# A fused retention and gated MLP kernel: first block loaded and masked by pairs of heads, third and fourth block prepared at other places

## The chip, the cores and the metric

The kernel runs on one core of one Trainium2 chip. The metric is the device time of one execution in microseconds (us). The engines are named as the profile names them: PE is TensorE, DVE is VectorE, ACT is ScalarE, POOL is GpSimd, SP is SyncE, which here only issues DMAs. PE multiplies, the others copy, scale and round. Every engine works through its own instructions in order.

## The reference

```python
def _attn_ref(q, k, v):                       # (8, 8, 576, 64) each: batch, heads, sequence, head dim
    scores = scale * np.matmul(q, k.transpose(0, 1, 3, 2))
    gamma = 1.0 - 2.0 ** (-5.0 - np.arange(H, dtype=np.float32))
    rel = pos[:, None] - pos[None, :]
    Dmat = np.where(rel >= 0, gamma[:, None, None] ** rel[None, :, :], 0.0)
    ret = scores * Dmat[None, :, :, :]
    return np.matmul(ret, v).astype(np.float32)

def _moe_ref(x, w_in, w_out):                 # x: 4608 x 512, w_in: 512 x 2048, w_out: 2048 x 512
    h = x @ w_in
    g = h * np.cos(h)
    return (g @ w_out).astype(np.float32)
```

The heads' outputs are put side by side and are the rows `x` of the second function.

## The kernel before

**Blocks and windows.** The 4608 tokens are cut into 18 blocks of 256 tokens (`j`) for the attention, and into 9 windows of 512 tokens (`n`) for the MLP. The decay is split into a factor on q and one on k (`gq`, `gkp`, `gkc`), so that a plain triangular mask is left. For each block: SP loads q, k and v (`load`); q and k are scaled and rounded to bf16 (`scaled`, line 174); v is rounded (`round_v`, line 185); PE turns q and k (`transpose_pe`, line 225, for blocks 0 and 1, `turned`, line 210, for the rest) into PSUM, and ACT or DVE copy the result to `qkT` (lines 230, 216); PE forms the scores (lines 264, 302), DVE masks them (`masked`, lines 282, 311); PE forms the states that go on to later tokens (`sums_of`, lines 352, 335), which are added up in `s_all` and rounded in `sb` (line 394); PE forms the outputs from the block itself (`out_own`, line 420) and from the carried state (`out_carried`, line 447), and ACT rounds them into `x_of`.

**The MLP.** `mm1` (line 490) multiplies four tiles of `w_in` with the window, ACT takes the cosine (line 503), DVE multiplies (line 506). The second product of window 0 is written out in the loop over `order` (line 991); windows 1 to 8 use `mm2_seven` (line 610), which forms seven products in place of eight, and needs sums of weight quarters, `w_sums` (line 529, DVE), made once, during window 0.

**Order.** The order is written out by hand. The tile layer adds the semaphores, and each engine runs its list in this order. What matters here is the start and window 0:

- SP issues the loads of block 0 (k, q, v, 512 KB each), then k, q of block 1, and v of block 1 once its k has landed.
- POOL makes masks, issues the first quarter of `w_in` (a cast DMA), scales k of block 1, and then issues the other three quarters. `w_dma` lists the weight DMAs: 0 to 3 are `w_in`, 4 to 7 the quarters of `w_out`.
- Block 2's loads are held by `gate=w_dma[3]` until the last quarter of `w_in` has landed, block 3's by `gate=w_dma[6]`. The third quarter of `w_out` is held until the first has landed (`after(w_dma[-1], w_dma[4])`).
- In window 0 `mm1` runs eight groups. Group 0 and 3 need the first quarter of `w_in`, group 1 and 4 the second, 2 and 5 the third, 6 and 7 the last. The sums, outputs and carried part of block 1 lie between groups 0 and 2.
- The second product of window 0 has 64 steps. A list `todo` says ahead of which step something else is put in: the scaling of half of q of block 2 on DVE (20), its turning (28), its states and scores (40), the adding of its states (41), scaling of block 3 (`prep(3)`, 42, on POOL), weight sums (`w_sums`), block 2's outputs (54), block 3's turning (60). The product lies in banks "m" (two tiles, `two`), "n" and "st" of PSUM. Two tiles in "m" are copied out by ACT and DVE (line 1001) after step 55:

```python
for u in range(2 * (t == 1) if t < 2 else 1) if e == ET - 1 else ():
    ...
    (act, vec)[u % 2](ot[:, 0], pss[u])
```

The first group of window 1 writes bank "m" again (`banks_of[1]` begins with "m"). It can begin when both copies are done.

`warm(n, tag)` (line 235) runs n matmuls on zeros into a bank; nothing reads them.

Of the kernel before, what the change touches and what calls it, by code (L numbers as in the profile page):

```python
# [17 lines left out]
def kernel(  # L18
# [113 lines left out]
    def load(j, names="qkv", gate=None):  # L132
# [27 lines left out]
            tiles["f" + name, j] = f  # L160
        return i

    def scaled(eng, j, name, y):
        f = tiles["f" + name, j]
        if ("qks", j) not in tiles:
            tiles["qks", j] = nat.tile([P, 2, 2, HG, 2, D], BF16, tag="qks", name="qks")
        dst = tiles["qks", j][:, "qk".index(name), y]
        if name == "q" or j < NP_B:
            src = f[:, :, y, :]
            by = (gq if name == "q" else gkp)[:, j % PERQ, y, :]  # L170
        else:
            src = f[:, y]
            by = gkc[:, (2 * j + y) % PERK, :]
        return eng.tensor_tensor(  # L174
            out=dst.rearrange("p b a d -> p a b d"),
            in0=src.rearrange("p (a b) d -> p a b d", a=2),
            in1=by.rearrange("p (a b) -> p a b", a=2).unsqueeze(3).to_broadcast([P, 2, HG, D]),
            op=ALU.mult,
        )
# [5 lines left out]
            runs[y](vb[:, y], f[:, :, y, :] if j < NP_B else f[:, y])  # L185
        tiles["vb", j] = vb

    def prep(j):
        for name in "kq" if j < NP_B else "qk":
            for y in range(2):  # L190
                scaled(nc.gpsimd, j, name, y)

    def new_qkT(j):
        tiles["qkT", j] = nat.tile([P, 2, 2, HG, P], BF16, tag="qkT", name="qkT")
# [23 lines left out]
    def transpose_pe(j, name, bank, evac, ys=(0, 1)):  # L218
        if ("qkT", j) not in tiles:
            new_qkT(j)  # L220
        m = "qk".index(name)
        ps = psum.tile([P, len(ys), HG, P], BF16, tag=bank, name="tr")
        for u, y in enumerate(ys):
            for hg in range(HG):
                nc.tensor.transpose(
                    ps[:, u, hg, :],
                    tiles["qks", j][:, m, y, hg].rearrange("s a d -> s (a d)"),
                    ident,
                )
        evac(tiles["qkT", j][:, m, ys[0] : ys[-1] + 1], ps)  # L230

    def warm(n, tag):
        ps = psum.tile([P, 512], F32, tag=tag, name="idle")
        for _ in range(n):
            nc.tensor.matmul(ps, lhsT=zeros[:, :P], rhs=zeros, start=True, stop=True)
# [10 lines left out]
            return cols  # L246
        return cols.rearrange("p (r i) -> p r i", r=2)[:, :, c.i0 : c.i0 + n]

    def scores(j, banks):
        cs = chunks[j]  # L250
        kT = tiles["qkT", j]
        ret = retp.tile([P, 2, HG, 2, P], BF16, tag="ret", name="ret")
        if cs[0].pair:
            pss = [
                psum.tile([P, HG, 2, P], F32, tag=t, name="sc")
                if isinstance(t, str)
                else [psum.tile([P, HG, P], F32, tag=u, name="sc") for u in t]
                for t in banks
            ]
            order = [(c, y, he, hg) for hg in range(HG) for y in range(2) for he in range(2) for c in cs]  # L260
            mask = mask_p
            for c, y, he, hg in order:
                ps = pss[he]
                nc.tensor.matmul(
                    ps[y][c.rows, hg, :] if isinstance(ps, list) else ps[c.rows, hg, y, :],
                    lhsT=kT[he * D : he * D + D, 1, y, hg, c.rows],
                    rhs=q_cols(c, he, hg, c.n),
                    start=True,
                    stop=True,
                )  # L270

            def masked(he):
                if isinstance(pss[he], list):
                    for y in range(2):
                        nc.vector.tensor_tensor(
                            out=ret[:, he, :, y, :],
                            in0=pss[he][y],
                            in1=mask[:, y].unsqueeze(1).to_broadcast([P, HG, P]),
                            op=ALU.mult,
                        )  # L280
                    return
                nc.vector.tensor_tensor(  # L282
                    out=ret[:, he].rearrange("p b r i -> p b (r i)"),
                    in0=pss[he].rearrange("p b r i -> p b (r i)"),
                    in1=mask.rearrange("p r i -> p (r i)").unsqueeze(1).to_broadcast(
                        [P, HG, 2 * P]
                    ),
                    op=ALU.mult,
                )
        else:  # L290
            ret = ret.rearrange("p a b r i -> p (a b r i)")[:, : 2 * HG * P].rearrange(
                "p (a b y i) -> p a b y i", a=2, b=HG, y=2
            )
            if isinstance(banks[0], str):
                both = psum.tile([P, 2, HG, 2, HP], F32, tag=banks[0], name="sc")
                ps = [both[:, he] for he in range(2)]
            else:
                ps = [psum.tile([P, HG, 2, HP], F32, tag=t, name="sc") for t in banks[0]]
            for hg in range(HG):
                for c in cs:  # L300
                    for he in range(2):
                        nc.tensor.matmul(  # L302
                            ps[he][c.rows, hg, c.y, :],
                            lhsT=kT[he * D : he * D + D, 1, c.y, hg, c.rows],
                            rhs=q_cols(c, he, hg, c.n),
                            start=True,
                            stop=True,
                        )

            def masked(he):  # L310
                nc.vector.tensor_tensor(  # L311
                    out=ret[:, he].rearrange("p b y i -> p (b y) i"),
                    in0=ps[he].rearrange("p b y i -> p (b y) i"),
                    in1=mask_c.unsqueeze(1).to_broadcast([P, H, HP]),
                    op=ALU.mult,
                )

        tiles["ret", j] = ret
        return [lambda: masked(0), lambda: masked(1)]

    def sums_of(j, bank):
# [399 lines left out]
    def load_next(**kw):  # L721
        nonlocal loaded
        if loaded < NB:
            load(loaded, **kw)
            loaded += 1
# [31 lines left out]
            out=at, in0=at, in1=lng.unsqueeze(1).to_broadcast(list(at.shape)), op=ALU.mult  # L757
        )

    load(0, "kqv")  # L760
    k1 = load(1, "k")
    load(1, "q")
    load(1, "v", gate=k1)
# [19 lines left out]
            kpos_i[p0:, c0:c1, :], pattern=[[P, c1 - c0], [0, H]], base=base, channel_multiplier=1  # L783
        )
    nc.vector.memset(zeros, 0.0)
    warm(11, "n")
    for h in range(H):
        nc.vector.memset(lng[:, h : h + 1], math.log(gammas[h]))
    nc.vector.memset(ln_scale, math.log(scale))
# [34 lines left out]
        )  # L824
    vec, act = nc.vector.tensor_copy, nc.scalar.copy

    scaled(nc.vector, 0, "k", 0)
    scaled(nc.vector, 0, "k", 1)
    transpose_pe(0, "k", "n", act, (0,))
    transpose_pe(0, "k", "st", act, (1,))  # L830
    scaled(nc.vector, 0, "q", 0)
    scaled(nc.vector, 0, "q", 1)
    transpose_pe(0, "q", "a", act, (0,))
    transpose_pe(0, "q", "b", vec, (1,))
    w_dma = [load_w_in(0)]
    round_v(0, (act, act))
    warm(2, "m")
    for masked in scores(0, "ab"):
        masked()
    sums_of(0, "st")()()  # L840
    scaled(nc.gpsimd, 1, "k", 0)
    warm(3, "m")
    transpose_pe(1, "k", "n", act, (0,))
    scaled(nc.gpsimd, 1, "k", 1)
    w_dma += [load_w_in(e) for e in (512, 1024, 1536)]
    load_next(names="kqv", gate=w_dma[3])
    ps0 = psum.tile([P, DG, BK], F32, tag="m", name="ov")
    out_own(0, ps0)
    scaled(nc.vector, 1, "q", 0)
    scaled(nc.vector, 1, "q", 1)  # L850
    transpose_pe(1, "k", "st", vec, (1,))
    out_carried(0, ps0)
    act(x_of(0), ps0)
    nc.scalar.activation(sine, half_pi, ACTF.Sin, bias=0.0, scale=1.0)
    round_v(1, (act, nc.gpsimd.tensor_copy))
    warm(2, "n")
    transpose_pe(1, "q", "a", vec, (0,))
    transpose_pe(1, "q", "b", vec, (1,))
    warm(2, "n")
    for masked in scores(1, "ab"):  # L860
        masked()
    w_dma += [load_w_out(e) for e in (0, 4)]
    w_dma.append(load_w_out(8))
    after(w_dma[-1], w_dma[4])
    for y in range(2):
        scaled(nc.gpsimd, 2, "k", y)
    w_dma.append(load_w_out(12))
    scaled(nc.gpsimd, 2, "q", 0)
    load_next(names="kqv", gate=w_dma[6])
    load_next()  # L870
    prepared = 4

# [48 lines left out]
    for n in range(NT):  # L921
# [37 lines left out]
        if n == 0:  # L959
# [3 lines left out]
            pss += [psum.tile([P, DM], F32, tag=t, name="o") for t in ("n", "st")]  # L963
            todo = [
                (20, lambda: scaled(nc.vector, 2, "q", 1)),
                (28, lambda: turned(2, "a", (act, vec))),
                (28, lambda: round_v(2)),
                (40, lambda: adds.append(states_and_scores(2, "a", "b"))),
                (41, lambda: adds.pop()()()),
                (42, lambda: prep(3)),  # L970
                (57, load_next),
                (55, lambda: round_v(3, (act, act))),
                (54, lambda: outputs(2, "b")),
# [2 lines left out]
            todo += [  # L976
                (at, lambda x=x, e=e: w_sums(x, e, e + 4))
                for at, x, e in (
                    (2, 5, 0), (8, 5, 4), (34, 6, 0), (35, 4, 0), (36, 7, 0),
                    (51, 6, 4), (52, 4, 4), (53, 7, 4),  # L980
                )
            ]
# [136 lines left out]
```

## Time and profile before

| | us |
|---|---|
| median of 3 runs | 297.07 (296.99 to 297.41) |
| the profiled execution's own time | 296.85 |
| its span in the profile | 295.1 |

| engine | busy us | share of the span | instructions |
|---|---|---|---|
| PE | 284.5 | 96% | 4367 |
| DVE | 215.2 | 73% | 300 |
| ACT | 170.5 | 58% | 200 |
| POOL | 143.4 | 49% | 163 |

The profiled execution is 1.75 us longer than its span and 0.22 us shorter than the median. A time in the profile counts from the span's start. A busy PE includes the idle matmuls of `warm`. "L490" is line 490 of the kernel before.

### The profile page before, as it was taken

Reading aid. Unit: us, or ns where it says so; the run is one execution under the profiler, and the core shown is the slowest. Engines: PE = TensorE matmul, PEld = TensorE weight load, DVE = VectorE, ACT = ScalarE, POOL = GpSimd, SP = SyncE. Lnnn points to the kernel's source line nnn. Section 1 sums busy time; section 2 is a strip of 40 time slices with the busy share of each in tenths; the row PEclk is TensorE's granted clock in tenths of the full one; section 3 lists DMA queues with packets and bytes.
Section 4 is the critical chain, followed back from the end, with each engine's and each line's share of the span. In section 5 each row is a group of like instructions: output and inputs, shape, how many; then the busy total and the mean of one; then the engine's idle time right before and its main releaser. Section 6 shows DMA issues by size and latency. Waiting matters only on the chain.

```text
span 295.1 us, 10506 instructions
## 1 busy us (share of the span) xinstructions
PE 284.5 (96%) x4367; PEld 196.3 (67%) x4388; DVE 215.2 (73%) x300; ACT 170.5 (58%) x200; POOL 143.4 (49%) x163
## 2 busy tenths in 40 slices
PE   7899999999999999999999999999999999999994
PEld 2578545878864687468745884588458845884584
DVE  5756767758857887698769866986698669745943
ACT  3676317476558844767476737674768466535620
POOL 8621439970585995349434942495249014102400
PEclk9999999999999999999999999999999999999999
DMA  7999999999989857833873396429201130112013
GB/s 222 289 206 224 227 251 233 260 231 221 227 189 232 218 134 173 201 71 98 213 189 77 78 225 176 100 52 257 58 0 40 38 73 0 40 47 62 2 36 107
DMA packets 103981, 42.62 MB, mean 144 GB/s; under 512 B 68480, under 2 KB 103424, under 8 KB 103936
## 3 DMA queue, kind: packets, MB, share of 16 engines
q1 hardware_dynamic: 99184, 37.37, 51.8%
q0 software_dynamic: 4224, 4.19, 8.7%
q8 instruction: 36, 0.59, 0.9%
q10 hardware_dynamic: 528, 0.39, 0.4%
q14 instruction: 9, 0.07, 0.1%
HBM read 36.70 MB, written 9.44 MB: 156 GB/s over the span
## 4 chain that ended last, share of the span: by engine, by line
PE 83%; DVE 5%; ACT 3%; DMA 3%; POOL 2%; SPq 1%; issue 1%; ACTq 0%; DVEq 0%
PE h L490 41%; PE o L610 32%; PE ov L420 3%; PE tr L210 2%; POOL qks L174 2%; DMA fq<-in_q_dram 2%; PE ov L447 1%; PE sc L302 1%; DMA fk<-in_k_dram 1%; DVE gT L506 1%; PE st L335 1%; ACT cosh L503 1%; SPq L153 1%; DVE qks L174 1%; DVE ret L282 1%
## 5 line engine op out<-in xcount | busy, mean ns | idle before, releaser
L490 PE MATMUL h<-xT,w_in_sb 128*128 128x512 bf16 (+1 forms) x689 | 126.8, 340 | 1.3 <-DVE qkT L216 0.4
L506 DVE TENSOR_TENSOR gT<-h,cosh 128x1024 bf16<-128x1024 f32 x72 | 87.7, 1222 | 33.5 <-ACT cosh L503 33.1
L490 PEld LDWEIGHTS <-w_in_sb 128*128 128x128 bf16 x704 | 68.1, 98 | 55.2 <-issue 1.1
L503 ACT ACTIVATE cosh<-h,half_pi 128x1024 f32<-128x1024 f32 x72 | 79.9, 1115 | 40.5 <-PE h L490 40.5
L549 POOL TENSOR_TENSOR gs<-gT 128x512 bf16<-128x512 bf16 x28 | 35.8, 1277 | 100.4 <-DVE gT L506 100.4
L610 PEld LDWEIGHTS <-gs 128*128 128x128 bf16 x528 | 49.7, 98 | 5.9
L610 PEld LDWEIGHTS <-gT 128*128 128x128 bf16 x384 | 36.6, 98 | 6.1
L636 DVE TENSOR_TENSOR ot<-ot,o 128x512 f32<-128x512 f32 x35 | 23.2, 683 | 22.4 <-ACT ot L640 14.2
L174 POOL TENSOR_TENSOR qks<-fk,gkc 128x512 bf16<-128x512 f32 x32 | 37.1, 1178 | 2.8 <-DMA fk<-in_k_dram 2.8
L174 POOL TENSOR_TENSOR qks<-fq,gq 128x512 bf16<-128x512 f32 x31 | 34.7, 1137 | 7.5 <-DMA fq<-in_q_dram 7.5
L216 ACT COPY qkT<-tr 128x1024 bf16<-128x1024 bf16 x29 | 27.7, 1022 | 6.4 <-PE tr L210 6.4
L394 ACT CAST sb<-s_all 128x768 bf16<-128x768 f32 (+2 forms) x18 | 16.3, 904 | 25.6 <-DVE s_all L384 21.6
L610 PE MATMUL o<-w_out_sb,gs 128*128 128x256 bf16 (+1 forms) x264 | 30.6, 269 | 0.1
L610 PE MATMUL o<-w_out_sb,gT 128*128 128x256 bf16 x256 | 30.6, 273 | 0.0
L610 PE MATMUL o<-ws,gs 128*128 128x256 bf16 (+1 forms) x264 | 30.5, 269 | 0.0
L640 ACT COPY ot<-o 128x512 f32<-128x512 f32 x33 | 19.3, 584 | 16.0 <-PE o L610 16.0
L311 DVE TENSOR_TENSOR ret<-sc,mask_c 128x512 bf16<-128x512 f32 x32 | 20.7, 685 | 7.3 <-PE sc L302 7.3
L185 POOL CAST vb<-fv 128x512 bf16<-128x512 f32 x31 | 19.3, 646 | 4.8 <-DMA fv<-in_v_dram 4.8
L466 ACT CAST xT<-ov 128x1024 bf16<-128x1024 f32 x16 | 16.2, 1012 | 9.4 <-PE ov L447 9.2
L384 DVE TENSOR_TENSOR s_all<-st,s_all 128x256 f32<-128x256 f32 x49 | 20.7, 422 | 1.2
L549 DVE TENSOR_TENSOR gs<-gT 128x512 bf16<-128x512 bf16 (+1 forms) x25 | 16.7, 668 | 0.5
L610 PE MATMUL o<-ws,gT 128*128 128x256 bf16 x128 | 15.3, 273 | 0.0
(73 smaller groups left out, 207.0 us busy)
## 6 DMA issues: line engine op xcount, KB each, us to landing
out_dram<-ot SPq DMA_DIRECT2D x68, 128.0 KB, 2.6
fk<-in_k_dram SPq DMA_DIRECT2D x28, 256.0 KB, 4.9
fv<-in_v_dram SPq DMA_DIRECT2D x28, 256.0 KB, 4.8
fq<-in_q_dram SPq DMA_DIRECT2D x12, 512.0 KB, 5.1
w_in_sb<-in_moe_w_in_dram POOLq DMA_DIRECT2D x4, 512.0 KB, 8.0
w_out_sb<-in_moe_w_out_dram POOLq DMA_DIRECT2D x4, 512.0 KB, 8.3
fq<-in_q_dram SPq DMA_DIRECT2D x4, 384.0 KB, 5.1
fk<-in_k_dram SPq DMA_DIRECT2D x2, 512.0 KB, 4.9
```

What stands on the lines that cost most here:

```text
L174: return eng.tensor_tensor(out=dst.rearrange("p b a d -> p a b d"), in0=src.rearrange("p (a b) d -> p a b d", a=2), in1=by.rearrange("p (a ...
L185: runs[y](vb[:, y], f[:, :, y, :] if j < NP_B else f[:, y])
L216: evacs[r](tiles["qkT", j][:, :, :, :, r * HP : r * HP + HP], pss[r])
L311: nc.vector.tensor_tensor(out=ret[:, he].rearrange("p b y i -> p (b y) i"), in0=ps[he].rearrange("p b y i -> p (b y) i"), in1=mask_c.unsqu ...
L384: nc.vector.tensor_tensor(out=s32[:, u], in0=ps[c.half][:, c.y], in1=s32[:, u - 1] if u else tiles["run"], op=ALU.add,)
L490: nc.tensor.matmul(ps[:, j, :], lhsT=w_in_sb[:, dg, (et + j) * P : (et + j + 1) * P], rhs=xT[:, dg, c0 : c0 + w], start=(dg == 0), stop=(d ...
L503: nc.scalar.activation(cosh, ps, ACTF.Sin, bias=half_pi, scale=1.0)
L506: nc.vector.tensor_mul(gT[:, et : et + m, c0 : c0 + w], ps, cosh)
L549: i = eng.tensor_tensor(out=tiles["gs", n, x][:, e : e + step], in0=a[:, e : e + step], in1=b[:, e : e + step], op=op_,)
L610: nc.tensor.matmul(dst[i], lhsT=lhs[:, e, j * P : (j + 1) * P], rhs=rhs[:, e, c0:c1], start=(fresh and e == 0 and (i == 0 or len(parts) > 2)),
L636: return lambda: nc.vector.tensor_tensor(out=out_, in0=in0, in1=in1, op=ALU.add)
L640: held.append(lambda ps=tiles["all", x]: nc.scalar.copy(t, ps))
```

## The change

- **Block 0 by pairs.** Its k and q come in eight DMAs of 128 KB in place of two of 512 KB: for pair `g` of head groups first k, then q, each as two DMAs. The order is k pair 0, q pair 0, k pair 1, q pair 1. Each is scaled in two DVE passes of 256 columns, turned by four transposes, copied by ACT. The scores and masks follow by pairs, too. One half of block 0's v is rounded on POOL in place of ACT.
- **Idle matmuls.** 8 in place of 11 at the start, and others moved.
- **Block 1.** Its transposes all come after the carried part of block 0, q's first half is copied by ACT.
- **Block 2.** Its loads are held until the third quarter of `w_in` (`w_dma[2]`) has landed, not the fourth. POOL issues the third quarter of `w_out` after it has scaled half of k of block 2, and the fourth after the other half; the wait for the first quarter of `w_out` falls away. Turning, rounding, scores and sums of block 2 stand four steps earlier in `todo`.
- **Block 3.** Its loads wait for the second quarter of `w_out` (`w_dma[5]`), not the third. Its q is scaled on DVE, four steps earlier; k stays on POOL.
- **Weight sums.** The three of steps 34 to 36 come at 37.2 to 37.6, so behind the masks and states of block 2 on DVE.
- Code for cases that don't arise falls away in `scores` and `prep`.

```diff
+    def load_heads(name, g):
...
+        for he in range(2):
+            h0 = he * HG + 2 * g
+            nc.sync.dma_start(
+                f[:, h0 : h0 + 2].rearrange("p h r d -> p h (r d)"),
+                src[0, h0 : h0 + 2, :BK, :].rearrange("h (p r) d -> p h (r d)", r=2),
+            )
+    def scaled_heads(eng, name, g):
...
+        for y in range(2):
+            eng.tensor_tensor(
+                out=dst[:, y],
+                in0=f[:, y],
+                in1=by[:, y, 2 * g : 2 * g + 2].unsqueeze(3).to_broadcast([P, 2, 2, D]),
+                op=ALU.mult,
+            )
+    def turned_heads(name, g, bank, evac=nc.scalar.copy):
...
+        for y in range(2):
+            for u in range(2):
+                nc.tensor.transpose(
+                    ps[:, y, u, :],
+                    tiles["qks", 0][:, m, y, 2 * g + u].rearrange("s a d -> s (a d)"),
+                    ident,
+                )
+        evac(tiles["qkT", 0][:, m, :, 2 * g : 2 * g + 2], ps)
-    def prep(j):
-        for name in "kq" if j < NP_B else "qk":
+    def prep(j, eng_q=nc.gpsimd):
+        for name in "qk":
             for y in range(2):
-                scaled(nc.gpsimd, j, name, y)
+                scaled(eng_q if name == "q" else nc.gpsimd, j, name, y)
-    def scores(j, banks):
+    def scores(j, banks, g0=0, g1=HG):
...
-    load(0, "kqv")
+    for g in range(2):
+        for name in "kq":
+            load_heads(name, g)
+    load(0, "v")
     k1 = load(1, "k")
...
-    warm(11, "n")
+    warm(8, "b")
...
-    scaled(nc.vector, 0, "k", 0)
-    scaled(nc.vector, 0, "k", 1)
-    transpose_pe(0, "k", "n", act, (0,))
-    transpose_pe(0, "k", "st", act, (1,))
-    scaled(nc.vector, 0, "q", 0)
-    scaled(nc.vector, 0, "q", 1)
-    transpose_pe(0, "q", "a", act, (0,))
-    transpose_pe(0, "q", "b", vec, (1,))
+    scaled_heads(nc.vector, "k", 0)
+    turned_heads("k", 0, "n")
+    scaled_heads(nc.vector, "q", 0)
+    warm(1, "b")
+    turned_heads("q", 0, "st")
+    scaled_heads(nc.vector, "k", 1)
+    warm(1, "b")
+    turned_heads("k", 1, "m")
+    scaled_heads(nc.vector, "q", 1)
+    masks = scores(0, "ab", 0, 2)
+    turned_heads("q", 1, "n")
+    for masked in masks:
+        masked()
     w_dma = [load_w_in(0)]
-    round_v(0, (act, act))
     warm(2, "m")
-    for masked in scores(0, "ab"):
+    masks = scores(0, "ab", 2, HG)
+    round_v(0, (nc.gpsimd.tensor_copy, act))
+    for masked in masks:
         masked()
+    warm(2, "m")
     sums_of(0, "st")()()
     scaled(nc.gpsimd, 1, "k", 0)
-    warm(3, "m")
     transpose_pe(1, "k", "n", act, (0,))
     scaled(nc.gpsimd, 1, "k", 1)
     w_dma += [load_w_in(e) for e in (512, 1024, 1536)]
-    load_next(names="kqv", gate=w_dma[3])
+    load_next(names="kqv", gate=w_dma[2])
     ps0 = psum.tile([P, DG, BK], F32, tag="m", name="ov")
     out_own(0, ps0)
-    scaled(nc.vector, 1, "q", 0)
-    scaled(nc.vector, 1, "q", 1)
-    transpose_pe(1, "k", "st", vec, (1,))
     out_carried(0, ps0)
     act(x_of(0), ps0)
+    scaled(nc.vector, 1, "q", 0)
+    transpose_pe(1, "k", "st", vec, (1,))
+    transpose_pe(1, "q", "a", act, (0,))
+    scaled(nc.vector, 1, "q", 1)
+    transpose_pe(1, "q", "b", vec, (1,))
     nc.scalar.activation(sine, half_pi, ACTF.Sin, bias=0.0, scale=1.0)
     round_v(1, (act, nc.gpsimd.tensor_copy))
-    warm(2, "n")
-    transpose_pe(1, "q", "a", vec, (0,))
-    transpose_pe(1, "q", "b", vec, (1,))
-    warm(2, "n")
     for masked in scores(1, "ab"):
         masked()
     w_dma += [load_w_out(e) for e in (0, 4)]
-    w_dma.append(load_w_out(8))
-    after(w_dma[-1], w_dma[4])
     for y in range(2):
         scaled(nc.gpsimd, 2, "k", y)
-    w_dma.append(load_w_out(12))
+        w_dma.append(load_w_out(8 + 4 * y))
     scaled(nc.gpsimd, 2, "q", 0)
-    load_next(names="kqv", gate=w_dma[6])
+    load_next(names="kqv", gate=w_dma[5])
...
                 (20, lambda: scaled(nc.vector, 2, "q", 1)),
-                (28, lambda: turned(2, "a", (act, vec))),
-                (28, lambda: round_v(2)),
-                (40, lambda: adds.append(states_and_scores(2, "a", "b"))),
-                (41, lambda: adds.pop()()()),
-                (42, lambda: prep(3)),
+                (24, lambda: turned(2, "a", (act, vec))),
+                (24, lambda: round_v(2)),
+                (36, lambda: adds.append(states_and_scores(2, "a", "b"))),
+                (37, lambda: adds.pop()()()),
+                (38, lambda: prep(3, nc.vector)),
...
-                    (2, 5, 0), (8, 5, 4), (34, 6, 0), (35, 4, 0), (36, 7, 0),
+                    (2, 5, 0), (8, 5, 4), (37.2, 6, 0), (37.4, 4, 0), (37.6, 7, 0),
                     (51, 6, 4), (52, 4, 4), (53, 7, 4),
```

## The prediction

> **What bounds the kernel now.** I read the page first: PE is busy 96% of the span, so only its gaps and the work that is not product can go. Windows of time show where they are (columns: stretch, length, then busy us and instructions of PE, PEld, DVE, ACT, POOL; clock; DMA share; GB/s).
>
> ```profile
> 2.50:3.00 0.50, 0.50 (x3) 0.21 (x2) 0.37 (x2) 0.00 (x0) 0.36 (x3) 1.00 0.62 156
> 32.00:48.00 16.00, 15.20 (x224) 7.53 (x226) 11.94 (x17) 4.73 (x6) 8.26 (x9) 1.00 1.12 244
> 48.00:64.00 16.00, 14.85 (x268) 11.74 (x269) 10.47 (x14) 10.55 (x13) 13.87 (x16) 1.00 1.02 242
> 116.00:146.00 30.00, 29.89 (x488) 20.47 (x488) 24.35 (x34) 18.94 (x22) 16.42 (x16) 1.00 0.61 147
> ```
>
> From about 66 us on PE has no gaps to speak of (29.89 of 30). The change ends before that, so its whole worth is how much earlier or later PE gets there. A shift made before 66 stays to the end.
>
> The chain of waits gives the only wait of window 0's second product that another engine sets:
>
> ```profile
> 43.28 4.95 POOL qks L174 x4
> 48.27 0.29 PE tr L210 x8
> 48.56 0.97 PE o L991 x4
> 49.53 1.37 PE h L490 x12
> ```
>
> POOL scales block 3; the last transposes wait 0.35 us for it; then window 1 begins at 49.44. What else window 1 needs is DVE's copy out of bank "m". DVE's timeline ahead of it:
>
> ```profile
> 39.56 0.69 DVE L216 COPY qkT<-tr 128x1024 bf16<-128x1024 bf16 x1 [2.91 <-ACT qkT L216]
> 40.17 1.58 DVE L529 TENSOR_TENSOR ws<-w_out_sb,ws 128x1024 bf16<-128x1024 bf16 x2
> 41.66 0.68 DVE L529 TENSOR_TENSOR w_out_sb<-w_out_sb 128x1024 bf16<-128x1024 bf16 x1
> 42.27 1.28 DVE L311 TENSOR_TENSOR ret<-sc,mask_c 128x512 bf16<-128x512 f32 x2
> 43.46 0.41 DVE L380 COPY s_all<-st 128x256 f32<-128x256 f32 x1
> 43.91 0.88 DVE L384 TENSOR_TENSOR s_all<-st,s_all 128x256 f32<-128x256 f32 x2
> 44.71 2.60 DVE L529 TENSOR_TENSOR ws<-w_out_sb,ws 128x1024 bf16<-128x1024 bf16 x2
> 47.24 1.53 DVE L529 TENSOR_TENSOR w_out_sb<-w_out_sb 128x1024 bf16<-128x1024 bf16 x1
> 48.69 0.69 DVE L1001 COPY ot<-o 128x512 f32<-128x512 f32 x1
> ```
>
> Two things are to be seen. DVE has no gap from 39.56 to 49.38, and 49.38 is when PE goes on: this queue is as late as POOL's, though the chain names only one of them. And a weight sum takes 0.68 to 0.8 us while POOL rests, but 1.3 to 1.5 from 44.71 on, while POOL scales.
>
> At the start I read SP's own timeline and POOL's:
>
> ```profile
> 0.80 0.43 SPq L139 DMA_DIRECT2D fk<-in_k_dram  x1
> 1.29 0.57 SPq L139 DMA_DIRECT2D fq<-in_q_dram  x1
> 1.91 1.28 SPq L139 DMA_DIRECT2D fv<-in_v_dram  x1
> ```
> ```profile
> 9.42 2.04 POOL L174 TENSOR_TENSOR qks<-fk,gkp 128x512 bf16<-128x512 f32 x2 [1.46 <-ACT vb L185]
> 11.41 2.29 POOL L742 DMA_DIRECT2D w_in_sb<-in_moe_w_in_dram x3
> ```
>
> By the times to landing, block 1's k arrives at 3.23 + 6.0 = 9.2; that (not ACT's v, which the wait is put down to) starts POOL at 9.42. Behind it stand the three DMAs of `w_in`; the second and third quarter land at 11.41 + 7.2 = 18.6 and about 12.2 + 8.9 = 21.1. PE needs them at 19.0 (group 1) and 21.3 (group 2; its predecessor's cosine starts at 21.41). So the slack of `w_in` is 0.4 and 0.2 us: however early block 0 is done, PE can't gain more than 0.2 us by group 2 unless `w_in` itself lands earlier.
>
> **The start, step by step.** A load's issue costs SP much the same whatever its size: 0.43 and 0.57 us for 512 KB above, 0.37 for block 1's v into an empty queue, and no less than 0.45 for any of 128 or 256 KB later. With a gap of 0.06, eight issues take 8 x 0.49 = 3.9 us, and v of block 0 is issued at 4.7 in place of 1.91. The DMA engines reach 345 to 350 GB/s about 1.85 us after the first issue (156 GB/s in 2.5 to 3.0). Two blocks of 512 KB then take 3.05 us, up to 5.7; v's data can't start before 4.7 + 1.85 = 6.55. So everything behind comes up to 0.85 us later. With 0.37 per issue (0.43 with the gap) it is 0.4, with 0.57 it is 2.0, and without a lag it is nothing. I take 0.6, since the rows of an empty queue (0.37, 0.43) are the nearest and a running queue's lag should be shorter than the first. Block 1's k then lands at 9.8, POOL scales it from 10.0 to 12.05, `w_in` lands at 19.2 and 21.7. Group 2 starts at 21.7 in place of 21.3: +0.4 us. Bounds: -0.2 (no delay) to +1.8 (2.0 later).
>
> Does block 0 itself hold PE? The last pair lands at about 6.7; two DVE passes (0.75), four transposes (0.40), ACT's copy (0.55), half the scores (0.35), two masks of 512 columns (1.38, by line 311's 0.69) end at 10.2, where the masks ended at 11.77. But in PE's list the transposes of block 1's k stand ahead of `out_own(0)`. They wait for POOL's first half, 10.0 + 1.04, so `out_own` starts at 11.45 and not at 10.2. Most of the 1.5 us is lost in this queue. From there block 1 needs the carried part, transposes (now behind it), DVE's scaling and copy, and scores: 11.45 + 0.95 + 0.3 + 0.4 + 0.45 + 0.65 + 0.4 + 0.45 + 0.65 = 15.7 for the first product, which began at 15.52. `w_in` sets the end, not this.
>
> Gates: block 2's loads start 2 us earlier, but the DMA engines are busy without a break from 3 to 40 us (share above 1), so they move beside the weights rather than ahead of them. The last quarter of `w_in` is needed at 28 and landed at 23.6; `w_out` by quarters at 31.7, 35, 39.4 and 44. The third, now behind block 2's k on POOL (about 29 + 6.9 = 36), keeps its date; the fourth comes no later than now. These edits I cost at nothing; without that slack each us of lateness would be one of PE's.
>
> **Window 0's second product.** Turning and scores four steps earlier neither add nor remove PE work. Gains: the carried state is ready before `out_carried` (0.2 us of wait at 45.4), and block 3's turning no longer waits (0.35). PE could begin window 1 at 49.44 + 0.4 - 0.55 = 49.3.
>
> DVE can't follow. The scores end four steps (4 x 0.2275 = 0.9 us) earlier, at 40.95 + 0.4 = 41.35. From there DVE has, in order: two masks 1.20, states 1.25, three weight sums 2.1 (0.69 each; POOL is idle then), q of block 3 1.35 (two passes, as the 1.28 of block 1), three weight sums, the copy 0.7. Earlier the first three sums ran before the masks, in time that PE needed anyway; now DVE idles there for 1.6 us (from the end of its copy of `qkT`, 39.35). The last three sums cost 2.1 if POOL rests, 4.06 as now if it scales throughout. They start at 47.25; block 4's q lands at 48.0 now, some tenths earlier when block 3's loads are not held. So POOL joins during the first of them: I take 3.2. The copy ends at 41.35 + 1.20 + 1.25 + 2.1 + 1.35 + 3.2 + 0.7 = 51.15, which is 1.7 us behind 49.44. Bounds by the two prices of the sums: 50.05 and 52.0.
>
> **Sum.** Prologue and second product together are +1.7, since DVE's lateness contains the 0.4. The profiled execution took 296.85 (its span of 295.1 and 1.75 around it), which gives 298.55; the median shown is 0.22 above that execution. I say 298.6.
>
> **Rivals.** (a) *DVE's copy is in time* (not slower). Place: the first group of window 1. If the copy ended before 48.7, PE would take the 0.55 and, with undelayed loads, the 0.2: 296.1. It decides from the point at which DVE's list is 0.95 us shorter than my cheapest sum without the delay (49.65). For it speaks that DVE's idle 1.6 us leaves room if the masks come earlier than I think; against it that the sum uses uncontended rows already. 0.15 for this and what lies near it.
> (b) *POOL rests while the sums run*: the copy at 50.05, 297.45, within 0.2% of now. Block 4's q would have to land after 49; it lands at 48.0 now with more ahead of it. With undelayed loads it would be 296.85. 0.23.
> (c) *Small DMAs are cheap to issue.* Mechanism: the loads keep their dates, the start gives -0.2, and DVE's lateness alone is left: 1.7 - 0.6 = +1.1, so 297.95. Against it stand SP's rows; 0.17. The Trainium skill ("DMA: Bandwidth & Descriptors", section "Anatomy of one DMA — SWDGE (gpsimd) path") puts a sequencer's dispatch at about 50 ns and calls descriptor generation small, for the GpSimd path; by it eight issues would cost 0.4 us and this rival would hold. The trace's 0.37 to 0.57 us per issue disagree, and they decide.
> (d) *Nothing of the pairing is seen*: masks no earlier than 11.77 because of late pieces. Then `out_own` moves to 11.8, the first product to 16.1, still hidden by `w_in` within 0.2 us. It changes the sum by nothing and is part of the forecast.
> The forecast itself, with POOL beside the sums for one to three of them and a delay of 0.3 to 1.0, has 0.45.
>
> **Numbers.** 0.2% (0.6 us) is about what a measurement of this kernel can tell from no change. Faster by more than that: (a), 0.15. The same: (b), 0.23. Slower: (c) and the forecast, 0.62. The range reaches down to (a), 296.0, and up to the dearest issues with my price of the sums, 296.85 + 1.8 + 1.3 = 299.95, so 299.9 (full contention with my delay gives 296.85 + 2.6 = 299.45). The forecast with (c) alone has 297.7 to 299.9.
>
> **What would show it.** In the profile after: SP's issue of block 0's v near 4.7; block 1's k landing 0.3 to 1 us later; masks of block 0 ending near 10.2 but `out_own` near 11.4; PE waiting for `w_in` ahead of group 2; DVE's list from 41.3 to 51 with q of block 3 in it, and PE idle ahead of window 1's first group, waiting for DVE. The prediction is wrong if v is issued before 4, if PE's wait for POOL ahead of block 3's turning is gone and none for DVE replaces it, or if the weight sums at the end take 0.7 each.

## The result, and the profile after

The changed kernel takes 309.25 us (median of four, 308.10 to 310.01); the kernel before took 297.24 beside it (296.99 to 298.28). The ratio is 1.0394 (1.0352 to 1.0435). Slower was the likeliest direction, but the forecast was +1.5 us against the median and the result is +12.0, far outside the range. The profiled execution of after took 309.44, with a span of 307.5, against 295.1. Executions of some kernels below fall into two groups some per cent apart; medians hold all of them, ratios leave the longer group out, and the profiles of e10, e11 and e12 are of the longer group.

The page's tenths of the granted clock show two dips; in the kernel before all 40 slices are 9:

```profile
PEclk9959999779999999999999999999999999999999
```

A slice is 7.7 us: the clock was low around 15 to 23 and around 54 to 69. The chain of waits (start, length, what) names what lies there:

```profile
6.02 10.12 DMA fq<-in_q_dram
...
20.14 3.53 PE h L520 x16
...
26.81 11.46 PE h L520 x104
...
58.46 0.61 DVE ot L1036
59.11 2.71 PE h L520 x12
...
76.26 4.53 PE h L520 x40
```

Set against the chain of before (its lines are L490 there), the loss builds up in four steps and then stays:

| point | before | after | later by | added |
|---|---|---|---|---|
| first product begins (PE's timeline) | 15.52 | 20.07 | 4.55 | 4.55 |
| unbroken row of 104 matmuls begins | 20.40 | 26.81 | 6.41 | 1.86 |
| window 1 begins | 49.53 | 59.11 | 9.58 | 3.17 |
| row of 40 matmuls begins | 64.01 | 76.26 | 12.25 | 2.67 |
| span | 295.1 | 307.5 | 12.4 | 0.15 |

**Step 1, a late load.** SP's timeline, start and length:

```profile
4.88 0.47 SPq L139 DMA_DIRECT2D fv<-in_v_dram  x1
5.39 0.58 SPq L139 DMA_DIRECT2D fk<-in_k_dram  x1
6.02 2.03 SPq L139 DMA_DIRECT2D fq<-in_q_dram  x1
```

Issue is as forecast: two pieces of 128 KB take 0.95 to 0.99 us, and block 0's v is issued at 4.88 (forecast 4.7). The landing is not. The issues of the first 14 us, with KB each and median us to landing:

```profile
fk<-in_k_dram SPq DMA_DIRECT2D x4, 128.0 KB, 2.5
fk<-in_k_dram SPq DMA_DIRECT2D x1, 512.0 KB, 6.1
fq<-in_q_dram SPq DMA_DIRECT2D x1, 512.0 KB, 10.1
```

Block 1's k lands at 5.39 + 6.1 = 11.5, in place of 9.2, and its q at 16.1, in place of 10.7. Meanwhile the engines moved 225 GB/s in 4 to 6 us and 240 in 6 to 8, where the kernel before moved 345 and 347. And at 6.81 POOL issued the first quarter of `w_in`, on its old date (7.02 before). The queues' rows for 10 to 12 us (packets, MB, share of the engines; q0 is POOL's, q1 SP's) show the cast moving while q still waits:

```profile
q0 software_dynamic: 282, 0.29, 93.4%
q1 hardware_dynamic: 287, 0.14, 26.3%
```

**Steps 2 and 4, the clock.** Stretches of after, cut where the clock changes (length; busy us and instructions of PE, PEld, DVE, ACT, POOL; granted clock; DMA share; GB/s):

```profile
10.47:13.89 3.42, 2.01 (x75) 1.56 (x76) 0.89 (x2) 1.94 (x4) 2.52 (x4) 1.00 1.18 228
13.89:17.30 3.41, 1.25 (x26) 0.77 (x14) 1.13 (x3) 1.01 (x1) 2.02 (x3) 0.50 1.17 284
54.85:58.26 3.41, 0.81 (x4) 0.29 (x3) 3.38 (x3) 2.28 (x3) 3.41 (x4) 1.00 0.95 251
58.26:61.67 3.41, 2.56 (x12) 1.57 (x11) 1.40 (x3) 0.00 (x0) 3.41 (x5) 0.50 0.91 206
```

PE rests, and what follows runs at half rate. The clock falls at 13.89, behind a stretch in which PE was busy 59%; most of its idle time there is a wait of 1.14 us for POOL's scaling of block 1's k, which started late because k landed late. The late q holds PE only after that (2.16 us, 14.76 to 16.92); this rest, in the next row, did not cause the first fall, but keeps PE little busy while the clock is low. The clock is back at 24.13. In between 16 matmuls take 3.53 us in place of 1.85 (1.68 of the 1.86 of step 2). The second fall, at 58.26, comes 2.6 us into PE's wait ahead of window 1. Behind it the first 12 matmuls of window 1 take 2.71 in place of 1.47, the next 24 4.12 in place of 2.79: together 2.57 of the 2.67 of step 4.

**Step 3, DVE's list.** DVE's timeline ahead of window 1, and who waits:

```profile
51.98 2.14 DVE L214 TENSOR_TENSOR qks<-fq,gq 128x512 bf16<-128x512 f32 x2
54.04 2.97 DVE L559 TENSOR_TENSOR ws<-w_out_sb,ws 128x1024 bf16<-128x1024 bf16 x2
56.93 1.52 DVE L559 TENSOR_TENSOR w_out_sb<-w_out_sb 128x1024 bf16<-128x1024 bf16 x1
58.38 1.28 DVE L1036 COPY ot<-o 128x512 f32<-128x512 f32 x2
59.11 2.71 PE L520 MATMUL h<-xT,w_in_sb 128*128 128x256 bf16 x12 [3.45 <-DVE ot L1036]
```

### The profile page after: what moved, and what is told of

Its sections match the earlier page's. It is cut to its first block, busy times and chain, and to the rows that moved or that the text cites. A ratio compares the mean times of both kernels' runs of the same rounds, so it can differ in the third digit from the quotient of the medians.

```text
span 307.5 us, 10530 instructions
## 1 busy us (share of the span) xinstructions
PE 291.5 (95%) x4382; PEld 198.8 (65%) x4382; DVE 217.1 (71%) x306; ACT 171.3 (56%) x201; POOL 142.2 (46%) x162
## 4 chain that ended last, share of the span: by engine, by line
PE 84%; DVE 7%; DMA 3%; ACT 3%; SPq 2%; issue 1%; DVEq 0%; ACTq 0%
PE h L520 41%; PE o L640 31%; DMA fq<-in_q_dram 3%; PE o L1026 3%; PE ov L450 2%; PE tr L250 2%; PE sc L332 1%; DVE ws L559 1%; PE ov L477 1%; SPq L170 1%; PE st L365 1%; DVE qks L214 1%; DVE ret L341 1%; DVE s_all L414 1%; DVE gT L536 1%; ACT cosh L533 1%
## 5 line engine op out<-in xcount | busy, mean ns | idle before, releaser
L520 PE MATMUL h<-xT,w_in_sb 128*128 128x512 bf16 (+1 forms) x704 | 132.1, 349 | 4.1 <-DVE ot L1036 3.4
L520 PEld LDWEIGHTS <-w_in_sb 128*128 128x128 bf16 x704 | 70.1, 101 | 61.1 <-issue 5.4
L214 POOL TENSOR_TENSOR qks<-fk,gkc 128x512 bf16<-128x512 f32 x32 | 37.2, 1179 | 19.2 <-DMA fk<-in_k_dram 19.2
L214 POOL TENSOR_TENSOR qks<-fq,gq 128x512 bf16<-128x512 f32 x29 | 32.6, 1142 | 6.4 <-DVE w_out_sb L559 5.3
L341 DVE TENSOR_TENSOR ret<-sc,mask_c 128x512 bf16<-128x512 f32 x32 | 20.7, 685 | 10.7 <-PE sc L332 9.7
L670 ACT COPY ot<-o 128x512 f32<-128x512 f32 x33 | 19.2, 583 | 16.0 <-PE o L640 16.0
L225 POOL CAST vb<-fv 128x512 bf16<-128x512 f32 x32 | 20.3, 658 | 4.1 <-DMA fv<-in_v_dram 4.1
L496 ACT CAST xT<-ov 128x1024 bf16<-128x1024 f32 x16 | 16.2, 1012 | 10.4 <-PE ov L477 10.2
```

What stands on the lines that cost most here:

```text
L214: return eng.tensor_tensor(out=dst.rearrange("p b a d -> p a b d"), in0=src.rearrange("p (a b) d -> p a b d", a=2), in1=by.rearrange("p (a ...
L341: nc.vector.tensor_tensor(out=ret[:, he].rearrange("p b y i -> p (b y) i"), in0=ps[he].rearrange("p b y i -> p (b y) i"), in1=mask_c.unsqu ...
L520: nc.tensor.matmul(ps[:, j, :], lhsT=w_in_sb[:, dg, (et + j) * P : (et + j + 1) * P], rhs=xT[:, dg, c0 : c0 + w], start=(dg == 0), stop=(d ...
L670: held.append(lambda ps=tiles["all", x]: nc.scalar.copy(t, ps))
```

## The experiments

The theory after this comparison: the pieces delay block 1's k and q into the cast of `w_in`; the rest that this leaves halves PE's clock; and DVE's list, in the new order, is late ahead of window 1 and halves it again. The first rival: the new order alone does it, and the pieces are hidden.

**e1_big_loads.** The changed kernel with the old loads of block 0.

```diff
-    for g in range(2):
-        for name in "kq":
-            load_heads(name, g)
-    load(0, "v")
+    load(0, "kqv")
```

> The changed kernel with k and q of block 0 again in one DMA of 512 KB each; everything else of the change stays. Theory (the eight pieces make the loads late, and the late loads cause the start's loss): block 1's q lands near 10.7 as before instead of 16.1, the first product begins at 15 to 15.5 instead of 20.1 at full clock, group 2 at about 21.1 (before 21.3). Of the 12.4 us of span some 6.4 go; what is left is DVE's late copy ahead of window 1, 1.2 to 2.2 us, and a lower clock behind it if PE rests for over 3 us. Time 298.2 to 300. Rival (the treatment by pairs itself, its order of transposes on PE, costs the start): the first product stays later than 17 and the time above 303.

Measured 299.46 us (ratio 1.0018, 0.9972 to 1.0064). The pieces carry 309.25 - 299.46 = 9.8 us; against the median of e1's six executions under 300 us (298.6) it is 10.7. In the profiled execution (298.27) the clock does not fall, DVE's sums take 0.7 each, PE waits 0.60 for the copy. The first product begins at 16.77, missing the expected 15 to 15.5: three of the four groups of block 1's transposes now stand behind the carried part (the first half of k stands ahead of `out_own`, at 12.04, so not all of them, as the list of the change has it), and DVE's second half of q behind a copy that waits for them. The row of 40 matmuls begins at 65.20, so that the rest of the change costs 1.2 in this execution.

**e2_pieces_only.** The kernel before with the eight pieces and nothing else.

```diff
-    load(0, "kqv")
+    for g in range(2):
+        for name in "kq":
+            load_heads(name, g)
+    load(0, "v")
```

> The kernel before with only one edit: k and q of block 0 come in the eight DMAs of 128 KB, in the order of the change. Theory: block 1's q lands at 15 to 16, the first product begins 4 to 5 us later and at half clock, group 2 is 5 to 6.5 us late; DVE's list in window 0 is that of before and adds nothing. Time 302 to 303.5. Rival of the prediction (the pieces cost only the 0.4 that it gave them): 297.3 to 297.8.

Measured 301.53 (ratio 1.011, 1.003 to 1.019), somewhat below the expected 302 to 303.5. Block 1's q lands at 16.2, as in the changed kernel, so this is the pieces' doing. But the first product, at 19.15, runs at full clock, and not at the expected half. PE's timeline shows what it does at that time:

```profile
16.05 0.61 PE L247 MATMUL idle<-zeros 128*128 128x512 bf16 x2
16.98 0.40 PE L237 MATMUL tr<-ident,qks 128*128 128x128 bf16 x4 [0.33 <-DVE qks L186]
...
17.82 0.59 PE L247 MATMUL idle<-zeros 128*128 128x512 bf16 x2
...
19.15 1.92 PE L502 MATMUL h<-xT,w_in_sb 128*128 128x256 bf16 x16
```

The old order has idle matmuls between block 1's steps; the change has none there, and the same late q lets PE rest for 2.16 us ahead of those transposes. The clock fell in this kernel, too, but earlier (7.84 to 11.25, behind a stretch with PE busy 42%), and was full again before these blocks. At the row of 40 matmuls this kernel is 3.74 late, e1 1.19; their sum is 4.9, the changed kernel 12.25. The rest is neither's alone.

**e3_copies_first.** The changed kernel with the last three weight sums put behind DVE's copy.

```diff
-                    (51, 6, 4), (52, 4, 4), (53, 7, 4),
+                    (56.2, 6, 4), (56.4, 4, 4), (56.6, 7, 4),
```

> The changed kernel with the last three weight sums behind DVE's copy out of bank m (steps 56.2 to 56.6 in place of 51 to 53). Theory (these sums, slowed by POOL, hold the copy, and the wait then lowers the clock): the 3.4 us of wait ahead of window 1 and the 2.7 us of half clock behind it go, time 303 to 304. Rival (the delay is handed on because PE then waits for other things, the second copy or the scores of block 3): 306 or more.

Measured 305.78 (ratio 1.0279, 1.0206 to 1.0351): 3.5 back, between theory and rival. The wait ahead of window 1 and the second half-rate stretch are gone, but the sums are still between DVE's two copies, and the scores of block 3 wait 2.36 us for the second one. In the profiled execution 1.0 us is gained ahead of the row of 104 matmuls already (25.84), where this kernel is the changed one: there block 1's q took 9.3 us.

**e4_warm.** The changed kernel with idle matmuls where PE rests: five, nine and two at the start, 15 ahead of window 1.

```diff
     sums_of(0, "st")()()
+    warm(5, "m")
...
     transpose_pe(1, "k", "st", vec, (1,))
+    warm(9, "n")
...
     scaled(nc.vector, 1, "q", 1)
+    warm(2, "n")
...
                     stores.append((u * P, ot))
+            warm(15, "b")
```

> The changed kernel with idle matmuls where PE waits: 5 behind the states of block 0, 11 around the turning of block 1's q, 15 ahead of window 1's first group. The waits stay. Theory (the granted clock falls because PE rests): the granted clock stays at 1.00, the first product's 16 matmuls take 1.9 instead of 3.5 us, window 1's first group runs at full rate; the time falls by 3.5 to 4.5 us, to 304.7 to 305.7. Rival (the clock falls for another cause, for instance the load of the DMA engines): the clock falls as before and the time is 309 or more.

Measured 305.44 (ratio 1.0262, 1.0196 to 1.0327), 3.8 less than the changed kernel. Nothing but idle matmuls was added, and the first product takes 1.92 us though it begins later still (20.82):

```profile
16.00:20.00 4.00, 3.69 (x47) 2.12 (x47) 2.03 (x4) 2.09 (x4) 2.03 (x3) 1.00 1.21 208
60.00:64.00 4.00, 3.66 (x63) 3.14 (x62) 3.04 (x4) 2.23 (x2) 3.38 (x5) 1.00 1.03 254
```

The loads are as late as before (block 1's q takes 9.6 us). So the clock follows how busy PE is, and not the loads. The expected 1.00 throughout was missed: the clock had fallen at 8.31, ahead of all added matmuls, behind a stretch with PE busy 64%, and came back at 15.13, behind one with PE busy 3.41 of 3.41 us.

**e5_w_in_held.** The changed kernel with the first quarter of `w_in` held until block 1's k has landed.

```diff
-    w_dma = [load_w_in(0)]
     warm(2, "m")
...
     round_v(0, (nc.gpsimd.tensor_copy, act))
+    w_dma = [load_w_in(0)]
+    after(w_dma[0], k1)
```

> The changed kernel with the first quarter of w_in held until block 1's k has landed (and issued behind POOL's half of block 0's v). Theory (the quarter's cast DMA takes the DMA engines from block 1's loads, which the pieces have made late): block 1's k lands at 9.9 to 10.3 and its q at 11.3 to 12.3 instead of 16.1, the first product begins at 16 to 17 instead of 20.1, at full clock; the time falls by 3 to 5 us to 304.5 to 306.5. Rival (SP's issues and the queue alone make q late): q still lands at 15 or later, and the time is 309 or more, since w_in is later too.

Measured 305.41 (ratio 1.0244, 1.0194 to 1.0293). Block 1's q, issued at 6.01, now takes 6.3 us and lands at 12.3 in place of 16.1: the collision is shown. Of the 3.8 us gained there the first product keeps 0.8 (19.24), since POOL issues the cast ahead of k's scaling, DVE's first half of q takes 2.33 us beside that scaling, and the clock is 0.50 again: it falls at 12.15, before q could hold PE, behind a stretch with PE busy 58%. So the expected start at 16 to 17 and at full clock was missed, and the expected time was met by another way: window 1 begins 2.9 us earlier (56.23, a wait of 2.27 us for the copy), and the row of 40 matmuls 4.0 (72.28).

**e6_q3_on_pool.** The changed kernel with block 3's q scaled on POOL again.

```diff
-                (38, lambda: prep(3, nc.vector)),
+                (38, lambda: prep(3)),
```

> The changed kernel with q of block 3 scaled on POOL again. Theory of the prediction (the two passes on DVE make its copy late): the copy out of bank m ends 1.3 to 2.1 us earlier relative to the second product's start, the clock does not fall behind it, time 304 to 307. Rival (the weight sums behind the masks and POOL's share are what makes it late, and POOL is now busier): the wait stays above 2.5 us and the time within 1 us of 309.

Measured 307.45 (ratio 1.0345, 1.0323 to 1.0367), 1.8 less: between what the two expected. The wait for the copy falls only from 3.45 to 2.60, because the last three sums still take 1.5 each beside POOL. The clock falls behind this wait, too (0.50 from 59.28 to 62.69), which the theory excluded.

**e7_window0_only.** The kernel before with the changes of window 0 alone (gates, order of `w_out`, earlier steps of block 2, block 3's q on DVE, the three sums later); the start is the old one.

```diff
+                (24, lambda: turned(2, "a", (act, vec))),
+                (24, lambda: round_v(2)),
+                (36, lambda: adds.append(states_and_scores(2, "a", "b"))),
+                (37, lambda: adds.pop()()()),
+                (38, lambda: prep(3, nc.vector)),
...
+                    (2, 5, 0), (8, 5, 4), (37.2, 6, 0), (37.4, 4, 0), (37.6, 7, 0),
```

> The kernel before with only the edits that lie behind the first product: gates and order of the weight quarters, steps of block 2 four earlier, q of block 3 on DVE, three weight sums behind the states. The start is that of before. The prediction's term for this is +0.2 to +2.2, most likely +1.3: 297.3 to 299.4, with PE waiting 0.8 to 2.5 us for DVE's copy ahead of window 1, and no wait for POOL ahead of block 3's turning. Rival (DVE is in time when the loads are not late): 296.3 to 297, no such wait.

Measured 298.75 (ratio 1.0045, 1.0026 to 1.0064): +1.7. This is the prediction's second term by itself, in DVE's, POOL's and PE's timelines:

```profile
48.22 1.41 DVE L529 TENSOR_TENSOR ws<-w_out_sb,ws 128x1024 bf16<-128x1024 bf16 x2
...
52.02 2.04 POOL L174 TENSOR_TENSOR qks<-fq,gq 128x512 bf16<-128x512 f32 x2 [6.47 <-DMA fq<-in_q_dram]
...
50.89 1.47 PE L490 MATMUL h<-xT,w_in_sb 128*128 128x256 bf16 x12 [1.03 <-DVE ot L999]
```

The last three sums took 0.7 each: POOL rested until 52.02, where it began on block 4's q at 48.18 in the kernel before. PE waits for the copy all the same.

**e8_q3_shared**, a try at something better: the kernel before with half of block 3's q on DVE, and one weight sum behind the copy.

```diff
-                (42, lambda: prep(3)),
+                (42, lambda: scaled(nc.vector, 3, "q", 0)),
+                (42.1, lambda: scaled(nc.gpsimd, 3, "q", 1)),
+                (42.2, lambda: [scaled(nc.gpsimd, 3, "k", y) for y in range(2)]),
...
-                    (51, 6, 4), (52, 4, 4), (53, 7, 4),
+                    (51, 6, 4), (52, 4, 4), (56.5, 7, 4),
```

> A try at a version better than both: the kernel before with half of block 3's q scaled on DVE and the other half on POOL, and the last weight sum behind the copy out of bank m. POOL ends block 3's k 1 us earlier, so the 0.35 us of wait ahead of its turning should go, and DVE's copy should be 0.1 to 0.8 us earlier. Expected 0.2 to 0.4 us faster than before: 296.7 to 297. If the second copy, now behind the last weight sum, holds the scores of block 3, it is even or 0.5 us slower.

Measured 297.57 (ratio 1.0028, 1.0000 to 1.0056): not faster. In its profile POOL got that half of q only at 45.56, and PE waited 0.28 and 1.16 us for POOL within block 3's turning, the longer time for k, which stands behind that half.

**e9_big_and_copies.** The loads of e1 with the sums of e3.

> The changed kernel with block 0's k and q in two loads of 512 KB, and with the last three weight sums behind DVE's copy out of bank m. With the two loads alone it took 299.46 us, and PE waited 0.6 us for that copy ahead of window 1. Theory (two independent costs: pieces at the start, DVE's list ahead of window 1): the 0.6 us wait goes, the first product stays near 16.8 and group 2 near 21.5, so 298.0 to 299.0, of which up to 1 us may return as a wait for the second copy inside window 1's first groups. Rival (what is left against the kernel before is all at the start, the order of the first product's scores): no change from 299.5. A version that beats the kernel before would be below 296.5.

Measured 303.70 (ratio 1.0188, 1.0139 to 1.0238): 4 us worse than e1, against both. Behind the copy the sums run beside POOL (4.2 us in place of 2.1) and hold DVE's second copy, for which PE waits inside window 1:

```profile
55.99 0.53 PE L332 MATMUL sc<-qkT 64*64 64x64 bf16 x31 [3.12 <-DVE ot L1033]
```

So e3 shows no better place for the sums: beside POOL they are slow in either place, and the wait moves. What e3 gained there is the clock, which did not fall a second time; here it does, behind this wait (0.50 from 56.17 to 59.58). Block 1's q took 9.35 us here from its issue at 4.97, where e1's took 5.9 and landed at 10.7: even with two loads q can be late.

**e10_four_loads** and **e11_two_queues.** The changed kernel with four loads of 256 KB (four heads each, k ahead of q), or with the eight pieces on two queues:

```diff
-        for he in range(2):
-            h0 = he * HG + 2 * g
-            nc.sync.dma_start(
-                f[:, h0 : h0 + 2].rearrange("p h r d -> p h (r d)"),
...
+        nc.sync.dma_start(
+            f[:, g * HG : (g + 1) * HG].rearrange("p h r d -> p h (r d)"),
...
```
```diff
-            nc.sync.dma_start(
+            (nc.scalar if name == "q" else nc.sync).dma_start(
```

> The changed kernel with block 0's k and q in four loads of 256 KB (four heads each) in place of eight of 128 KB. Theory (a load lands some 6 us after its issue, and SP issues one every 0.51 us, so block 1's loads are late by the time that SP spends on the pieces): block 0's v is issued near 2.9, block 1's k lands near 10 and its q, of which less is then left when the first quarter of w_in begins to move, near 12 to 14; the first product starts near 17.5 to 18.5, and the whole takes 301 to 304 us, between 299.5 with two loads and 309.25 with eight. Rival (any splitting makes the engines move less per us, whatever the issue): block 1's q lands near 16 as with eight, 307 us or more.

> The changed kernel with the four pieces of q issued on ACT's queue and the four of k on SP's: as many pieces of the same size, but SP issues four before block 0's v in place of eight. Theory (issue time on SP): v is issued near 2.9, the start is like that with four loads of 256 KB, 301 to 304 us, as far as ACT's own work at the start is not held up (it issues for about 2 us, before its first exponentials). Rival (the number or the size of the pieces sets the rate at which the engines move): block 1's q still lands near 16, 307 us or more.

e10: median 303.30 (ratio 1.0159, 1.0118 to 1.0200). e11: median 303.59; three executions at 300.1 to 300.8, three at 306.4 to 308.6; ratio 1.0099 (1.0073 to 1.0124). So halving what SP issues ahead of v takes 6 us off the median, as the theory said. But in e10's profile (304.73) block 1's q can be used only at 15.81, near the rival's 16 and not at 12 to 14, and the first product starts at 19.39; and half of e11's executions look like the rival's. One of those is the profiled one (307.24): block 1's q was issued at 4.71, exactly as in the kernel before, yet it took 10.6 us. The engines moved 265 and 289 GB/s in 4 to 6 and 6 to 8 us. The issue date alone does not set the landing. What the loads have moved by 10 us, about when the cast's data begin to move in these profiles, tells more: block 0 and block 1's k and q are 2.62 MB, of which 2.55 were moved by then in the kernel before and in e1, 1.99 in the changed kernel, 1.88 in e2, 2.09 in e10 and 2.07 in e11. What is left shares the engines with the cast.

**e12_two_queues_later_w_in.** e11 with the first quarter of `w_in` issued behind the first half of block 1's k on POOL.

```diff
-    w_dma = [load_w_in(0)]
...
     scaled(nc.gpsimd, 1, "k", 0)
+    w_dma = [load_w_in(0)]
```

> The kernel with the pieces on two queues, and with the first quarter of w_in issued on POOL behind the first half of block 1's k instead of ahead of block 0's v, so about 5 us later. There, block 1's q was issued at 4.71 us, as in the kernel before, and still landed 10.6 us later in the profiled execution. Theory (what moves ahead of that q is the cast of w_in; without it a load lands about 6 us after its issue): q lands by 11.5 and the first product starts between 16.5 and 18, with 299 to 301.5 us in every run. Rival (the pieces slow the engines whatever else moves): q lands after 14, first product after 18.5, some runs at 304 us or more.

Measured 303.41 (302.12 to 310.54; ratio 1.0197, 1.0169 to 1.0226). The row of q in the issues of the first 14 us, then PE's timeline:

```profile
fq<-in_q_dram SPq DMA_DIRECT2D x1, 512.0 KB, 6.9
```
```profile
19.21 3.59 PE L520 MATMUL h<-xT,w_in_sb 128*128 128x256 bf16 x16 [2.04 <-DMA w_in_sb<-in_moe_w_in_dram]
```

With no cast beside it q lands at 11.7, as the theory said (by 11.5); its time was missed all the same. In the profiled execution (310.54) the last scores of block 1 end at 17.2, and PE now waits until 19.21 for `w_in`. In this kernel the start is a budget of bytes: with q let through first, `w_in` is late.

## Why the prediction was wrong, and where it was right

- **Issue cost of small loads: right.** 0.48 us each, v at 4.88. Rival (c), cheap issues, is out.
- **"Everything behind comes up to 0.85 us later ... I take 0.6": this is the step that failed.** Block 1's k landed 2.3 later, its q 5.4. The step assumed that the DMA engines stay at 345 GB/s from 1.85 us on and only pause ahead of v. One 128 KB piece every 0.51 us (from the rows shown) is at most 257 GB/s, and 225 to 240 were measured, so that block 0 alone fell behind. Issue time is not all of it: on two queues the same working gives 514 GB/s, and e11's profile has 265 and 289. What else slows the pieces is open.
- **The collision was not in the sum at all.** The prediction followed k to POOL and `w_in`, but not q, and did not ask what POOL issues meanwhile. e5 and e12 show it: with the cast held, q takes 6.3 and 6.9 us in place of 10.1 and 10.6.
- **"`w_in` sets the end, not this": wrong here.** The first product came at 20.07 in place of 15.7, and group 1, for which `w_in` was to be there at 19.2, began at 25.42 without a wait for it. Only e12, where `w_in` was moved, waits for it.
- **Masks near 10.2, `out_own` near 11.4:** 11.36 and 13.05. That `out_own` waits for block 1's k on POOL and not for its masks was right; with k 2.3 late it cost more than forecast. e1 has 12.37 with the old loads, still 0.9 above the forecast, and there the order costs 1.2 at the first product.
- **No term for the clock.** Removed and moved `warm` calls were not costed. e2, with them, meets the same late q at full rate. By the rows, 1.68 and 2.57 us; by e4, 3.8 net. The Trainium skill ("TensorE: Matmul & The Clock Gate", section "Part 1: The HAM clock gate") has the clock fall to half after an idle window of about 3.4 us and rise after as long a busy one. The trace agrees on the length: the stretches at one clock last 10.24, 34.13 and 6.83 us (13.89, 24.13, 58.26, 65.09), whole multiples of 3.41. It does not agree that the window must be idle: PE was busy 59% of the one ahead of the first fall and 24% of the one ahead of the second.
- **DVE's list ahead of window 1: right that the copy comes late, and near in size by luck where it was alone.** +1.3 was forecast for it; e7 measured +1.7 by the medians. But the 3.2 us for the last three sums, with POOL beside them, were about 2.0: POOL rested, which is the condition of rival (b), and 0.7 for each sum is one of the prediction's own signs of being wrong. That was made up elsewhere in e7: block 2's scores ended 0.4 us earlier than before (41.37 for 41.79) and not 0.9, the first three sums took 2.7 in place of 2.1 beside POOL's k, and DVE waited 0.31 for block 3's q. In the changed kernel it cost 3.17: the start is 6.4 us late, but the loads of later blocks are not (POOL begins on block 4 at 52.07, in e7 at 52.02), so POOL scales block 4 during all of the last three sums (1.46, 1.42, 1.45) and q of block 3 (2.14 in place of 1.29). The prediction had full contention as a bound (4.06 for the three; 4.33 measured), and none for q. The Trainium skill ("SBUF — State Buffer", section "SBUF: two separate sides") calls the port pair that the two engines share an exclusive lock, held for a whole instruction, for a DVE operation with two SBUF inputs. The doubling agrees. Strict turns would make a sum and a POOL pass 0.69 + 1.02 = 1.71 us; 1.46 is measured.
- **Gates and `w_out` at nothing:** no wait of PE for `w_out` is in the chain. But block 4's q, forecast some tenths earlier than 48.0, was taken up only at 52.02 in e7. Which of the edits to the loads did this, no run separates.

The parts do not add up: pieces alone +3.7 and the rest alone +1.2 at the row of 40 matmuls, both together +12.25. The first loss of clock comes from late loads meeting an order without idle matmuls; the second from a late PE meeting a POOL that is not late. When the first comes differs: e3 and e6 have the changed kernel's code up to there, and their clocks fell at 16.03 and 11.49.

No version here beats the kernel before. What lets e11's shorter executions escape has no trace, and in e9 q was late although 2.55 MB had moved by 10 us.

## What to carry to other kernels

When loads are cut up, follow every load behind them to its landing, with the queue's issue pitch as a limit on the rate, and list what other queues begin to move on a date that does not shift. A matmul that nobody reads can be what pays for the next stage: when one is removed, price the next block at half clock and see how busy PE stays there. And two edits that each cost little should be costed together where one makes late what the other needs in time.

## What the runs showed of the hardware

- Loads of 128 KB were issued at the same pitch as ones of 512 KB (0.48 against 0.43 and 0.57 us for the first two) and landed after 2.5 to 2.8 us.
- A 512 KB load on SP's queue took 6 us to land, and 9.3 to 10.6 where POOL's cast DMA was under way; in 10 to 12 us the cast's queue had 93.4% of the engines' time, SP's 26.3%.
- From its first change on, the granted clock of all fourteen profiles is 1.00 or 0.50, and changes only whole multiples of 3.41 us apart. Ahead of its 18 falls before the end PE was busy 8 to 64% of the last 3.41 us. No stretch of this grid with 65% or more was followed by a fall, and three with less were not either (53, 56 and 64%). It came back behind stretches with PE busy 82 to 100%, though not behind every such one (97% in e12). In the changed kernel PE rested 1.14 us at most at a time ahead of the first fall (11.59 to 12.73), and the low clock lasted 10.24 us.
- A two-input pass over 1024 columns on DVE took 0.69 us alone and 1.42 to 1.52 beside POOL; two POOL passes 2.04 alone and 2.94 beside DVE.
